# A decode kernel's gate weights of layer 1: three loads of 3, 6 and 3 blocks in place of two of 6 and 6

## The chip, the cores and the metric

One core of one Trainium2 chip. The metric is the device time of one launch in microseconds (us), lower is better.

## The reference

Two layers, each an attention step for one token over the last 4096 positions of a cache (32 heads of 192), and a gated MLP. Both layers use the same weights.

```python
def _B_ref(x, w_gate, w_up, w_down):          # the part that the change touches
    g = jnp.einsum("bsd,df->bsf", x, w_gate)  # D = 640, F = 1536
    u = jnp.einsum("bsd,df->bsf", x, w_up)
    h = _sigmoid(g) * u
    return jnp.einsum("bsf,fd->bsd", h, w_down)

x = x + _A_ref(_layernorm(x), k_cache, v_cache, wq, wo)   # layer 1: attention
x = x + _B_ref(_layernorm(x), w_gate, w_up, w_down)       #          MLP
x = x + _A_ref(...)                                       # layer 2, same weights and cache
x = x + _B_ref(...)
```

## The kernel before

The kernel streams 218 MB from HBM through a large on-chip buffer. All its large loads are issued by SyncE, in one fixed order, on one queue. A load is issued once the instructions that read the old content of its place are done (a semaphore wait on SyncE); later loads wait behind it. So the queue is kept full as long as SyncE is released early enough.

Layer 1's MLP works in a region of cells, each of which holds one block: 128 of the 1536 columns of a weight (128 x 640 values of bfloat16, 160 KB). The gate needs cells 0 to 11, the first seven up blocks cells 12 to 18. The first down blocks and the rest of up are loaded over the gate's cells once the gate's matmuls have read them.

```python
# the gate's matmuls are done in four groups of three blocks: name: (first cell, first block, end block)
MW = {"wg0": (0, 0, 3), "wg1": (3, 3, 6), "wg2": (6, 6, 9), "wg3": (9, 9, 12), "u0": (12, 0, 2), "u1": (14, 2, 7),
      "d0": (0, 0, 3), "d1": (3, 3, 6), "u2": (6, 7, 10), "u3": (9, 10, 12), "d2": (11, 6, 9), ...}
# its loads, in the order in which they are issued: as MW, but the gate in two loads
MD = {"wg0": (0, 0, 6), "wg2": (6, 6, 12), **{k: v for k, v in MW.items() if k[0] != "w"}}
# which group of matmuls must be done before a load into its cells
MAFTER = {"d0": ("wg0",), "d1": ("wg1",), "u2": ("wg2",), "u3": ("wg3",), "d2": ("wg3", "u0"), ...}
# ... the program's order of loads around it:
seq += [("wol", 14), ("wol", 15)] + [(k,) for k in (*MD, "v1", "wq2", "v0", ...)]

# the MLP of layer 1 (cut)
for k in ("wg0", "wg1", "wg2", "wg3"):
    c, f0, f1 = MW[k]
    mark("done_" + k, proj(0, range(f0, f1), g_of, 0, rc[c:c + f1 - f0]))   # waits for the loads of these cells
ln_rstd(K2_MLP, eps_m, rstd_c, res("rstd"))
up("u0", "u1")
# ... sigmoid; then hT = gate * up for the first 7 blocks
down("d0", "d1"); up("u2", "u3")
# ... hT for the last 5 blocks
down("d2", "d3", "d4")
```

`wol14` and `wol15` are the last weights of the attention; `u1` (800 KB) is the last load before `d0`, the first one that has to wait for gate matmuls.

## Time and profile before

| | before |
|---|---|
| time, median of the first three runs | 513.68 us (513.53 to 513.91) |
| span of the profiled run | 512.2 us |
| mean DMA rate | 427 GB/s |
| first up pair landed / first down load issued | 279.80 us / 275.45 us |

The page of the kernel before. The first line is busy time in us, share of the span and instructions of each engine; the line DMA has one digit for each fortieth of the span, the busy share of the sixteen DMA engines in tenths (9 is 90% or more):

```profile
PE 262.5 (51%) x3716; PEld 138.4 (27%) x3716; DVE 101.5 (20%) x385; ACT 85.1 (17%) x171; POOL 4.3 (1%) x31
...
DMA  9999999999999999999999999999999999999996
...
DMA packets 9676, 218.47 MB, mean 427 GB/s; under 512 B 1208, under 2 KB 1592, under 8 KB 4664
```

Every slice but the last reads 9, and 218.47 MB at 427 GB/s make 511.6 us of the span's 512.2. That is the bound: the DMA engines never rest, so the time is the bytes, plus whatever makes an engine rest.

Next, the chain of waits of the kernel before around layer 1's MLP: start, duration, what.

```profile
260.92 18.89 DMA big<-in_wu_dram
...
279.85 0.84 PE scores L684 x25
...
280.71 5.40 DMA big<-in_wd_dram
```

The chain goes through "DMA" from the issue of the second up load at 260.92 to its landing at 279.80. This load did not take 18.9 us; it stood in the queue behind the others for most of them. A chain of waits through a full queue shows what waited, and not what could be made shorter.

The timeline of SyncE, which issues the loads (start, duration from the first to the last of the group, line, output and input, count). "wg" is the gate, "wu" up, "wd" down:

```profile
259.49 0.91 SPq L217 DMA_DIRECT2D big<-in_wg_dram  x2
260.44 0.91 SPq L217 DMA_DIRECT2D big<-in_wu_dram  x2
275.45 0.80 SPq L217 DMA_DIRECT2D big<-in_wd_dram  x2
277.74 0.81 SPq L217 DMA_DIRECT2D big<-in_wu_dram  x2
278.83 2.85 SPq L217 DMA_DIRECT2D big<-in_wd_dram  x3
```

And the timeline of TensorE in the same stretch; L684 is the gate's and up's matmuls, the square bracket gives the idle time before and what ended it:

```profile
274.86 0.96 PE L684 MATMUL scores<-sh,big 128*128 128x1 bf16 x30 [0.61 <-DVE bank L670]
277.15 0.96 PE L684 MATMUL scores<-sh,big 128*128 128x1 bf16 x30 [1.34 <-DMA big<-in_wg_dram]
277.97 0.56 PE L384 MATMUL bank<-sc 128*128 128x1 f32 x2
278.40 0.41 PE L684 MATMUL scores<-sh,big 128*128 128x1 bf16 x10
279.85 0.83 PE L684 MATMUL scores<-sh,big 128*128 128x1 bf16 x25 [1.05 <-DMA big<-in_wu_dram]
```

The gate runs in two bursts of 30 matmuls, one for each load. The first burst releases the first two down loads on SyncE, the second the next loads.

### The profile page before, as it was taken

How to read it: one execution, taken by the hardware profiler on the slowest of the kernel's cores; microseconds unless marked ns; L12 is line 12 of the kernel's file. 1: busy time of each engine (PE TensorE's matmuls, PEld its weight loads, DVE VectorE, ACT ScalarE, POOL GpSimd, SP SyncE). 2: the span in 40 equal slices, each digit the busy share in tenths (PEclk: the TensorE clock that was granted, in tenths of full speed). 3: DMA queues.
4: the chain of work that ended last, by engine and by line, in shares of the span. 5: the costliest groups of instructions: out<-in, count | busy, mean ns of one | idle time of the engine just before them, and what ended most of it. 6: DMA issues, size and time to landing. Idle time of an engine off the chain costs nothing.

```text
span 512.2 us, 8583 instructions
## 1 busy us (share of the span) xinstructions
PE 262.5 (51%) x3716; PEld 138.4 (27%) x3716; DVE 101.5 (20%) x385; ACT 85.1 (17%) x171; POOL 4.3 (1%) x31
## 2 busy tenths in 40 slices
PE   0352455344643254436566767774725344634565
PEld 0221222122311122222234424442312122312234
DVE  0221212112210221112121343231202112210311
ACT  1110111011100111011121024221211011101220
POOL 0010000000000000000000000000000000000000
PEclk9955665565566775566575578675655566555855
DMA  9999999999999999999999999999999999999996
GB/s 426 426 427 426 427 430 428 430 453 444 426 430 430 431 435 426 430 448 444 399 420 412 409 440 434 432 430 427 450 439 435 430 430 439 431 431 413 434 424 280
DMA packets 9676, 218.47 MB, mean 427 GB/s; under 512 B 1208, under 2 KB 1592, under 8 KB 4664
## 3 DMA queue, kind: packets, MB, share of 16 engines
q1 hardware_dynamic: 9512, 218.14, 99.2%
q8 instruction: 13, 0.21, 0.1%
q10 hardware_dynamic: 144, 0.06, 0.0%
q14 instruction: 7, 0.06, 0.0%
HBM read 218.20 MB, written 0.00 MB: 426 GB/s over the span
## 4 chain that ended last, share of the span: by engine, by line
DMA 64%; PE 22%; DVE 8%; ACT 3%; issue 2%; SPq 1%; DVEq 0%; POOL 0%; ACTq 0%; POOLq 0%
DMA big<-in_uc_dram 54%; PE scores L432 8%; DMA big<-in_wd_dram 6%; PE o L494 6%; DMA big<-in_wu_dram 4%; DVE sc L442 3%; PE bank L448 2%; ACT e_sb L458 2%; PE bank L414 2%; PE bank L529 1%; SPq L217 1%; PE bank L464 1%; ACT diag L445 1%; DVE sc L477 1%; DVE qs L420 1%
## 5 line engine op out<-in xcount | busy, mean ns | idle before, releaser
L432 PE MATMUL scores<-big,qs 128*32 128x512 bf16 x744 | 82.0, 608 | 10.3 <-DVE qs L420 9.6
L414 PE MATMUL bank<-sh,big 128*128 128x1 bf16 x465 | 17.0, 166 | 130.9 <-DMA big<-in_uc_dram 128.5
L494 PE MATMUL o<-big,et_sb 128*2 128x384 bf16 x1024 | 77.4, 471 | 8.5 <-DMA big<-in_uc_dram 4.2
L445 ACT ACTIVATE diag<-cst,sc 128x128 f32<-128x128 bf16 x32 | 12.8, 401 | 304.8 <-DVE sc L442 296.8
L442 DVE TENSOR_REDUCE sc<-scores 128x1 f32<-128x1024 f32 x31 | 37.9, 1224 | 77.8 <-PE scores L432 77.8
L414 PEld LDWEIGHTS bank<-sh,big 128*128 128x128 bf16 x465 | 14.6, 103 | 134.0 <-DMA big<-in_uc_dram 112.2
L448 PE MATMUL bank<-diag,sc 128*128 128x128 f32 x64 | 22.5, 447 | 46.7 <-ACT diag L445 46.7
L458 ACT ACTIVATE e_sb<-scores,sc 128x1024 bf16<-128x1024 f32 x31 | 37.4, 1205 | 42.1 <-DVE sc L453 39.9
L494 PEld LDWEIGHTS o<-big,et_sb 128*2 128x2 bf16 x1024 | 28.4, 107 | 44.2 <-issue 29.9
L420 DVE TENSOR_TENSOR qs<-bank,cst 128x96 bf16<-128x96 f32 x30 | 7.7, 258 | 159.6 <-PE bank L414 159.6
L432 PEld LDWEIGHTS scores<-big,qs 128*32 128x32 bf16 x744 | 24.3, 131 | 43.0 <-issue 29.5
L448 PEld LDWEIGHTS bank<-diag,sc 128*128 128x128 f32 x64 | 14.1, 276 | 72.7 <-ACT diag L445 70.4
L501 ACT CAST o_sb<-o 128x384 bf16<-128x384 f32 x64 | 29.7, 474 | 22.7 <-PE o L494 22.4
L529 PE MATMUL bank<-sh,big 128*128 128x1 bf16 x480 | 17.1, 165 | 14.9 <-DVE sh L518 14.9
L468 DVE CAST et_sb<-bank 128x64 bf16<-128x64 f32 x32 | 7.2, 225 | 71.1 <-PE bank L464 71.1
L529 PEld LDWEIGHTS bank<-sh,big 128*128 128x128 bf16 x480 | 14.5, 99 | 17.4 <-DVE sh L518 12.1
L449 DVE TENSOR_REDUCE sc<-bank 128x2 f32<-128x128 f32 x32 | 9.3, 292 | 43.3 <-PE bank L448 43.3
L464 PE MATMUL bank<-cst,e_sb 128*128 128x8 bf16 x256 | 11.7, 169 | 6.8 <-ACT e_sb L458 6.7
L464 PEld LDWEIGHTS bank<-cst,e_sb 128*128 128x128 bf16 x256 | 9.0, 102 | 23.0 <-issue 16.5
L475 PE MATMUL o<-sc 128*128 128x2 f32 x62 | 13.7, 291 | 0.6 <-ACT o_sb L501 0.6
L475 PEld LDWEIGHTS o<-sc 128*128 128x128 f32 x62 | 11.8, 239 | 2.0 <-ACT o_sb L501 1.3
L477 DVE RECIPROCAL sc<-o 64x1 f32<-64x1 f32 x62 | 10.2, 165 | 9.5 <-PE o L475 7.9
(80 smaller groups left out, 109.5 us busy)
## 6 DMA issues: line engine op xcount, KB each, us to landing
big<-in_uc_dram SPq DMA_DIRECT2D x20, 7104.0 KB, 22.6
big<-in_uc_dram SPq DMA_DIRECT2D x11, 3552.0 KB, 20.6
big<-in_uc_dram SPq DMA_DIRECT2D x2, 3072.0 KB, 18.6
big<-in_uc_dram SPq DMA_DIRECT2D x8, 480.0 KB, 7.4
big<-in_uc_dram SPq DMA_DIRECT2D x1, 2784.0 KB, 13.3
big<-in_uc_dram SPq DMA_DIRECT2D x1, 2304.0 KB, 10.7
big<-in_uc_dram SPq DMA_DIRECT2D x1, 2048.0 KB, 12.1
big<-in_wg_dram SPq DMA_DIRECT2D x2, 960.0 KB, 16.2
```

Of the source, the lines that this page charges most:

```text
L414: ins = t.matmul(qe[:, i:i + 1], lhsT=w[:, c * 2 * DH + c0:c * 2 * DH + c0 + P], rhs=xq[:, c:c + 1], start=(c == 0), stop=(c == DC - 1))
L432: ins = t.matmul(sc_x[1 + b][32 * j:32 * j + 32, :], lhsT=qs[:, y, k, :], rhs=slot(sa, WQE + k * W + (4 * b + j) * 512, 512), start=(k == ...
L442: pg.op("dve", lambda v: v.reduce_max(out=mx, in_=sc_x[0][:], axis=AX.X), wr=[res("mx")], ex=sc_x[3:5])
L445: pg.op("act", lambda a: a.mul(out=diag[:], in_=ident, mul=mx), rd=[res("cst"), res("mx")], wr=[res("diag")])
L448: pg.op("pe", lambda t: t.matmul(dmx[:, 0:P], lhsT=ones_f, rhs=diag[:], start=True, stop=True), rd=[res("diag"), res("ones")], ex=[rb[2]])
L458: pg.op("act", lambda a: a.activation(out=e_sb[:], in_=sc_x[0][:], func=ACT.Exp, bias=nbias, scale=srs_c, accum_out=rowsum), rd=[res("nbia ...
L464: ins = t.matmul(qe[:, 0:2 * NB].rearrange("p (r x) -> p r x", r=2)[:, :, 4 * b:4 * b + 4], lhsT=e_sb[:, b * P:(b + 1) * P], rhs=sel, star ...
L475: pg.op("pe", lambda t: t.matmul(sm, lhsT=ones_f, rhs=rs2[z], start=True, stop=True), rd=[res(f"rs2{z}"), res("ones")], wr=[res("rsum")], ...
L477: rb[bk].last["dve"] = pg.op("dve", lambda v, h=h: v.reciprocal(out=Rn[z][64 * h:64 * h + 64], in_=sm[64 * h:64 * h + 64, h:h + 1]), rd=[r ...
L494: ins = t.matmul(o8[h][32 * j:32 * j + 2, 0:2 * DH].rearrange("p (a d) -> p a d", a=2), lhsT=et_sb[:, z, h * NB + 2 * u:h * NB + 2 * u + 2 ...
L501: pg.op("act", lambda a, h=h: a.copy(out=o8_sb[:, :, h * DH:(h + 1) * DH], in_=o8[h][:, 0:2 * DH].rearrange("p (a d) -> p a d", a=2)), wr= ...
L529: ins = t.matmul(yT[:, j:j + 1], lhsT=wo[:, c * D + j * P:c * D + (j + 1) * P], rhs=oTb[z][:, c:c + 1], start=False, stop=(c == 2), skip_g ...
```

## The change

The first gate group (blocks 0 to 2) gets a load of its own, so that its matmuls can start as soon as 480 KB have landed, and the load that they release can be issued earlier. The middle six blocks, read by two groups of matmuls, come in one load, and the last three in another.

```diff
-    MD = {"wg0": (0, 0, 6), "wg2": (6, 6, 12), **{k: v for k, v in MW.items() if k[0] != "w"}}
+    MD = {"wg0": (0, 0, 3), "wg1": (3, 3, 9), "wg3": (9, 9, 12), **{k: v for k, v in MW.items() if k[0] != "w"}}
```

## The prediction

> **What bounds the kernel now.** The DMA engines. The page's DMA table gives 218.47 MB at a mean of 427 GB/s: 511.6 us of a 512.2 us span. Its slices show a DMA share of 9 in all but the last, while PE is busy 51%, DVE 20%, ACT 17%. The DMA packet records say it more sharply: from about 1 to 508 us at least fifteen, nearly always sixteen packets are in flight, also from 255 to 292 us, where the first layer's MLP runs. The largest packets (56,832 B in 2098 ns on one engine, 433 GB/s on sixteen) sit at the "fabric ceiling" of 435 GB/s that the Trainium skill gives ("DMA: Bandwidth & Descriptors", Specifications). The chain of waits shows PE 22% and DVE 8%, but it follows buffers coming free while the queue still holds earlier transfers; those shares can't be won.
>
> **What the change does.** Two gate loads of 960 KB (blocks 0-5, 6-11) of the first layer become 480, 960 and 480 KB (0-2, 3-8, 9-11). Bytes, destinations, arithmetic and matmul order stay. It adds one issue and one semaphore.
>
> 1. Earlier first block. In the list of DMA issues with landings, the first 960 KB land at 274.81 us, the second at 277.11. In the timeline the normalised input is ready near 274.5 and the gate matmuls start at 274.86. With 480 KB landing near 273.7, blocks 0-2 start near 274.5, and the first down load is issued near 275.1 instead of 275.45.
> 2. Blocks 3-5 now wait for the 960 KB piece, near 276.1: the second down load is issued near 276.6 instead of 275.85. The second pair of up loads goes out 0.4 to 0.7 us sooner; the last gate block ends near 277.75 instead of 278.1.
> 3. None of it is on the critical path. The first down load was issued 4.35 us before the transfer ahead of it landed (279.80); that is the smallest such margin among the MLP's released loads (others 4.4 to 6.6 us). Moving issues by -0.7 to +0.8 us never empties the queue. hT waits for the up load that lands at 279.80, behind the same bytes.
> 4. Cost. A packet of 3,840 B takes 149 ns, one of 7,680 B 291 ns: two small ones cost 7 ns more. On each engine eight packets of 7,680 B become sixteen of 3,840 B: 56 ns, plus one semaphore packet of 9 ns: +0.065 us on a saturated resource. The Trainium skill (same page, "Anatomy of one DMA") calls the semaphore write nearly free; 9 ns agrees.
> 5. The extra issue costs SyncE about 0.47 us near 260 us (spacing of neighbouring issues), 15 us before it could matter.
>
> **Predicted time:** 513.68 + 0.07 = 513.75 us, range 513.2 to 514.3 (the three runs spread over 0.4 us). Faster by over 2%: 0.005; within 2%: 0.99; slower: 0.005.
>
> **What would show it.** Right: gate landings near 273.7, 276.1 and 277.3; gate matmuls in three bursts; following up loads landing about 0.07 us later; sixteen packets in flight from 255 to 292 us; 256 more packets of 3,840 B and 128 fewer of 7,680 B. Wrong in step 3: packets in flight well below sixteen there. Wrong in step 4: landings drifting by several tenths.
>
> **What would make it wrong.** A chip with another DMA rate or wider spread; a queue that holds fewer loads than I think, so that one more outstanding load stalls SyncE; the granted clock falling differently in layer 2, so that a buffer comes free later than the queue's slack allows.

## More of the kernel before

Last, stretches of 1 us: for each engine its busy time, then the granted clock of TensorE, the mean busy share of the sixteen DMA engines (it can pass 1, since an engine's packets overlap a little), and GB/s:

```profile
core 0: us, PE busy (x) PEld busy (x) DVE busy (x) ACT busy (x) POOL busy (x), PEclk, DMA share, GB/s
...
277.00:278.00 1.00, 0.85 (x31) 0.85 (x31) 0.00 (x0) 0.00 (x0) 0.00 (x0) 0.50 0.99 401
278.00:279.00 1.00, 0.80 (x17) 0.72 (x13) 0.00 (x0) 0.40 (x2) 0.00 (x0) 0.50 0.99 405
279.00:280.00 1.00, 0.15 (x5) 0.15 (x6) 0.40 (x2) 0.34 (x2) 0.00 (x0) 0.50 1.02 417
280.00:281.00 1.00, 0.68 (x25) 0.59 (x23) 0.23 (x1) 0.00 (x0) 0.00 (x0) 0.50 1.14 362
```

The DMA share stays near 1 through the hand-over from gate to down loads. Single stretches waver in GB/s, but by the packet records at least fifteen packets are in flight at every moment from 255 to 292 us.

## The result, and the profile after

| | before | after |
|---|---|---|
| time, median of six runs | 513.63 us (513.21 to 513.99) | 513.75 us (513.35 to 514.30) |
| ratio | | 1.0003, 95% interval 0.999 to 1.0016 |
| span of the profiled run | 512.2 us | 513.0 us |
| gate landings | 274.81, 277.11 | 273.95, 276.24, 277.40 |
| first up pair landed | 279.80 | 280.13 |
| the four gate releases on SyncE: loads issued | 275.45, 275.85, 277.74, 278.14 | 275.44, 276.87, 277.27, 278.04 |

A ratio here is the mean time of one kernel's fast runs over that of the other's of the same rounds, so it is not quite the ratio of the medians quoted.

The time did not change: the interval goes from 0.1% faster to 0.16% slower. The changed kernel's profiled run happened to be its slowest (514.3 us); a later profile of it has a span of 511.9 us. In the first one the DMA engines were about 0.5 us late (mean of the sixteen) in the load issued at 208 us, well before the MLP, with a stretch near 61 us in which the packets in flight fell to 13. When its numbers are laid beside those of before, some 0.3 us are to be taken off in the MLP: the last attention weights had landed at 272.81 us in place of 272.52.

The page of the changed kernel:

```profile
PE 262.5 (51%) x3716; PEld 137.8 (27%) x3716; DVE 101.6 (20%) x385; ACT 84.8 (17%) x171; POOL 4.2 (1%) x31
...
DMA  9999999999999999999999999999999999999996
...
DMA packets 9820, 218.47 MB, mean 426 GB/s; under 512 B 1224, under 2 KB 1608, under 8 KB 4808
```

The busy times are the same, and the bytes are; there are 144 more packets, which are 128 of data (256 more of 3,840 B, 128 fewer of 7,680 B) and 16 semaphore writes.

Its chain of waits:

```profile
262.05 18.08 DMA big<-in_wu_dram
...
280.18 0.84 PE scores L684 x25
...
281.03 5.94 DMA big<-in_wd_dram
```

The same chain, with the same up load at its middle. The timeline of SyncE:

```profile
260.15 1.38 SPq L217 DMA_DIRECT2D big<-in_wg_dram  x3
261.57 2.69 SPq L217 DMA_DIRECT2D big<-in_wu_dram  x2
275.44 1.76 SPq L217 DMA_DIRECT2D big<-in_wd_dram  x2
277.27 1.09 SPq L217 DMA_DIRECT2D big<-in_wu_dram  x2
278.73 3.10 SPq L217 DMA_DIRECT2D big<-in_wd_dram  x3
```

Three gate loads; the first down load goes out at 275.44 (275.16 without the offset of this run; the second profile has 275.17), and the second not 0.4 but 1.43 us behind it. The timeline of TensorE:

```profile
274.87 0.54 PE L684 MATMUL scores<-sh,big 128*128 128x1 bf16 x15 [0.35 <-DVE sc L374]
276.29 0.96 PE L684 MATMUL scores<-sh,big 128*128 128x1 bf16 x30 [0.87 <-DMA big<-in_wg_dram]
277.45 0.56 PE L684 MATMUL scores<-sh,big 128*128 128x1 bf16 x15 [0.20 <-DMA big<-in_wg_dram]
277.87 0.56 PE L384 MATMUL bank<-sc 128*128 128x1 f32 x2
278.30 0.41 PE L684 MATMUL scores<-sh,big 128*128 128x1 bf16 x10
280.18 0.82 PE L684 MATMUL scores<-sh,big 128*128 128x1 bf16 x25 [1.48 <-DMA big<-in_wu_dram]
```

Three bursts of 15, 30 and 15 matmuls, as the diff says. The first starts when the normalised input is ready. Both timelines name DVE as its releaser, but in the kernel before the load landed at 274.81 us, 0.05 us before the first matmul, and here it landed at 273.95, 0.92 us before: the load is no longer what the burst waits for. The stretches of 1 us:

```profile
277.00:278.00 1.00, 0.80 (x26) 0.71 (x22) 0.00 (x0) 0.00 (x0) 0.00 (x0) 0.50 1.04 431
278.00:279.00 1.00, 0.70 (x13) 0.62 (x12) 0.00 (x0) 0.46 (x2) 0.00 (x0) 0.50 1.00 412
279.00:280.00 1.00, 0.00 (x0) 0.00 (x0) 0.40 (x2) 0.27 (x1) 0.00 (x0) 0.50 1.07 432
280.00:281.00 1.00, 0.82 (x25) 0.74 (x25) 0.00 (x0) 0.00 (x0) 0.00 (x0) 0.50 0.96 388
```

The DMA share stays near 1 (0.96 to 1.07), as before. Whatever the change did to the gate, the DMA engines did not notice.

### The profile page after: what moved, and what is told of

The parts are those of the page before. It is cut to its first block, busy times and chain, and to the rows that moved or that the text cites. A ratio compares the mean times of both kernels' runs of the same rounds, so it can differ in the third digit from the quotient of the medians.

```text
span 513.0 us, 8584 instructions
## 1 busy us (share of the span) xinstructions
PE 262.5 (51%) x3716; PEld 137.8 (27%) x3716; DVE 101.6 (20%) x385; ACT 84.8 (17%) x171; POOL 4.2 (1%) x31
## 4 chain that ended last, share of the span: by engine, by line
DMA 63%; PE 23%; DVE 7%; ACT 2%; issue 2%; SPq 1%; DVEq 0%; POOL 0%; ACTq 0%; POOLq 0%
DMA big<-in_uc_dram 54%; PE scores L432 8%; PE o L494 7%; DMA big<-in_wd_dram 6%; DMA big<-in_wu_dram 4%; DVE sc L442 3%; PE bank L448 2%; PE bank L414 2%; PE bank L529 1%; ACT e_sb L458 1%; PE bank L464 1%; SPq L217 1%; ACT diag L445 1%; DVE sc L477 1%; DVE qs L420 1%
```

## The experiments

Two theories of why the time stayed stood at first.

- **Theory A**: the DMA engines are saturated, and issues come early enough to keep them so. Shifting releases by under 1 us does nothing; only packets cost.
- **Theory B**: the chain of matmuls from the gate to the next layer sets the time, and the change's earlier first group and later second group cancel.
- A third, **theory C**, is that every load carries a fixed cost that the queue does not hide.

Each kernel was timed over five rounds, but for "one load, last" (three), beside the kernel before on the same chip.

| kernel | first down load issued, us | idle DMA time, 270 to 300 us | median | before | ratio (95%) |
|---|---|---|---|---|---|
| before | 275.45 | 0.01 | | | |
| changed, again | 275.17 | 0.01 | 513.78 | 513.88 | 0.9999 (0.9986 to 1.0013) |
| twelve loads | 274.82 | 0.00 | 513.86 | 513.88 | 1.0000 (0.9986 to 1.0014) |
| gate matmuls twice | 275.57 | 0.01 | 514.16 | 513.88 | 1.0004 (0.9991 to 1.0018) |
| three and nine | 275.44 | 0.11 | 513.71 | 514.16 | 0.9988 (0.9976 to 1.0001) |
| nine and three | 276.40 | 0.03 | 513.76 | 514.16 | 0.9990 (0.9977 to 1.0003) |
| gate matmuls four times | 276.96 | 1.74 | 517.69 | 513.90 | 1.0077 (1.0064 to 1.0091) |
| eleven and one | 277.26 | 0.41 | 515.07 | 514.16 | 1.0019 (1.0004 to 1.0034) |
| one load | 277.63 | 0.75 | 515.44 | 513.88 | 1.0032 (1.0018 to 1.0045) |
| one load, last | 280.77 | 3.28 | 518.03 | 514.16 | 1.0076 (1.0059 to 1.0093) |

"Idle DMA time" is worked out from the trace's packet records: the number of packets in flight at every moment, its shortfall below sixteen summed over time and divided by 16. It is a lower bound of what is lost: the mean number in flight of kernels that kept their time is 16.3 to 16.5 in this stretch, not 16, and a packet that takes longer than usual counts as work (the last experiment comes back to this).

### The changed kernel again

The same kernel as the change; no edit.

> The changed kernel itself, once more. Theory A (the DMA engines are saturated at every moment, so only their own packets cost time): 513.75 us within 0.4 us, ratio to the kernel before 1.0001. Theory B (the chain of matmuls from the gate to the next layer sets the time, and an earlier first block and later second block cancel): also about 1.000. This run is the control, and its trace tells whether the 0.65 us by which the first down load landed late in the first trace of the changed kernel is repeatable (it would be 1.8 us after the up load ahead of it again) or jitter between DMA engines (then about 1.2 us).

Measured: 513.78 us against 513.88, ratio 0.9999. Its first down load landed 1.12 us behind the up load ahead of it (280.99 and 279.87), so the 1.84 us of the first trace do not belong to the change. In the first trace the spread between the first and the last engine rose from 1.75 to 2.41 us at this load, and a fetch of instructions (a packet of 16,384 B, 0.93 us) lies there, at 279.82 us. Whether it held up the last engine can't be seen, since the records of packets do not name their engine. The four releases went out at 275.17, 276.59, 276.99 and 277.74 us.

### One gate load

```diff
-    MD = {"wg0": (0, 0, 6), "wg2": (6, 6, 12), **{
+    MD = {"wg0": (0, 0, 12), **{
```

> All twelve gate blocks in one load of 1920 KB, so that no gate matmul can start before about 277.1 us, 2.3 us later than before, and the first down load is issued near 277.7 us in place of 275.45. Theory A: eight packets of 15,360 B (573 ns) per engine in place of sixteen of 7,680 B (291 ns), 72 ns less, and one semaphore packet of 9 ns less: -0.08 us, ratio 0.9998; the smallest margin of a load's issue to the landing ahead of it falls from 4.35 to about 2 us, and at least fifteen packets stay in flight. Theory B: the gate's last block and what follows it end 1 to 2 us later, so +1 to +2 us, ratio 1.002 to 1.004.

Measured: 515.44 us against 513.88, ratio 1.0032: 1.6 us slower, where theory A expected 0.08 us faster and full queues. Theory B had the size right. But the stretches of 1 us say where the time went:

```profile
277.00:278.00 1.00, 0.96 (x36) 0.97 (x37) 0.00 (x0) 0.00 (x0) 0.00 (x0) 0.50 0.89 369
278.00:279.00 1.00, 1.00 (x32) 1.00 (x30) 0.00 (x0) 0.00 (x0) 0.00 (x0) 0.50 0.81 165
279.00:280.00 1.00, 0.77 (x22) 0.69 (x22) 0.00 (x0) 0.67 (x3) 0.00 (x0) 0.50 0.71 210
280.00:281.00 1.00, 0.55 (x21) 0.46 (x18) 0.63 (x3) 0.06 (x1) 0.00 (x0) 0.50 0.96 369
```

From 278 to 280 us the DMA engines moved 165 and 210 GB/s; the packet records fall to four in flight at 278.25. So it is idle DMA time after all, though SyncE issued the first down load at 277.63 us, 2.04 us before the load ahead of it landed (279.67).

The records of the semaphores explain it. A load adds 16 to its semaphore, one from each DMA engine when that engine's share is in; the Trainium skill says so ("DMA: Bandwidth & Descriptors", Why a DMA increments its semaphore by 16 and not by 1: the engines "finish independently"), and the trace has 16 separate times. For the up load ahead:

```
second up load, times of its 16 increments (us)   first    4th     8th    12th    13th    last
before                                           277.89  278.06  278.18  278.59  279.25  279.80
changed, again                                   277.95  278.16  278.28  278.53  279.46  279.87
one load                                         277.95  278.08  278.25  278.54  279.41  279.67
```

"Landed" is the last engine. Twelve of the sixteen had finished more than 1 us before it. The spread stays nearly the same from load to load (1.90 to 2.05 us for the loads that land from 262.95 to 282.16 us in the kernel before). The records do not name the engines, so it is inferred, and not seen, that an engine that is ahead stays ahead; that one runs dry first. In the kernel before, the first down load's packets begin at 277.58 us, which is when the first engine was through with the up load. And in "one load" the first down packets begin at 278.59, 0.96 us after their issue at 277.63. So the condition is: issue about 1 us before the first engine runs dry, that is by about 276.6 us.

- **Theory A2** therefore: as A, but a release has to come by 276.6 us; the margin of the kernel before is 277.58 - 275.45 - 0.96 = 1.17 us, not the 4.35 us that the prediction counted to the landing.

### Twelve gate loads

```diff
-    MD = {"wg0": (0, 0, 6), "wg2": (6, 6, 12), **{
+    MD = {**{f"wg{i}": (i, i, i + 1) for i in range(12)}, **{
```

> Twelve gate loads of 160 KB, one block each. Gate matmuls start as early as they can, and each block waits for 160 KB only. Theory A: 96 packets of 1,280 B (55 ns) per engine, 5280 ns, in place of 4656 ns, and ten semaphore packets of 9 ns more: +0.71 us, ratio 1.0014; the loads behind land about 0.7 us later. Theory B: no slower than before, perhaps 0.3 us faster, ratio 0.9994 to 1.0000. Theory C (every load carries a fixed cost of its own that the queue does not hide, of the order of 0.5 us as the issues on SyncE are spaced): +4 to +5 us, ratio 1.009.

Measured: 513.86 us against 513.88. Theory C is out: ten more loads cost nothing near 4 us. The 0.71 us of theory A lie at the edge of the interval (0.14% is 0.72 us), so the runs alone can't decide and the trace has to. Over the mean of the sixteen increments, the second up load comes 0.45 us later behind twelve loads than behind two, with the times just ahead of the gate loads as the zero; for the change itself it is 0.05 to 0.06 us in both of its traces. So packet durations, taken one by one, over-count: 0.45 of 0.71 us. The traces have 16.3 to 16.5 packets in flight on sixteen engines, so packets overlap a little; that this is what hides a part of each was not tested. SyncE was held up for 3.1 us at the fifth of these issues and for 2.5 at the sixth, with no cost, since the queue in front of the engines was long.

### Every gate matmul twice

```diff
-  mark("done_" + k, proj(0, range(f0, f1), g_of, 0, rc[c:c + f1 - f0]))
+  mark("done_" + k, proj(0, [*range(f0, f1)] * 2, g_of, 0, rc[c:c + f1 - f0]))
```

This is made from the changed kernel; the second pass overwrites the first with the same values.

> The changed kernel with every gate matmul done twice: 60 more matmuls of 128x1, about 0.54 us more for every three blocks, right result. The first down load is issued near 275.7, the last of the four gate releases near 279 to 280 us. Theory A: the added 2.2 us lie inside the margins of 4.35 us and more: ratio 1.000 (within 0.0007) to the kernel before. Theory B: +1 to +2 us, ratio 1.002 to 1.004.

Measured: 514.16 us against 513.88, ratio 1.0004: no effect that the runs can show, and the DMA idle time stayed at 0.01 us. Here is TensorE's timeline with each gate matmul done twice:

```profile
274.60 0.94 PE L684 MATMUL scores<-sh,big 128*128 128x1 bf16 x30 [0.35 <-DVE sc L374]
276.01 2.56 PE L684 MATMUL scores<-sh,big 128*128 128x1 bf16 x90 [0.48 <-DMA big<-in_wg_dram]
278.44 0.57 PE L384 MATMUL bank<-sc 128*128 128x1 f32 x2
```

and with one gate load, with SyncE's issue of its first two down loads:

```profile
277.04 1.76 PE L684 MATMUL scores<-sh,big 128*128 128x1 bf16 x60 [3.03 <-DMA big<-in_wg_dram]
278.66 0.56 PE L384 MATMUL bank<-sc 128*128 128x1 f32 x2
277.63 0.80 SPq L217 DMA_DIRECT2D big<-in_wd_dram  x2
```

The gate ends at 276.01 + 2.56 = 278.57 us in the first and at 277.04 + 1.76 = 278.80 us in the second. These are 0.23 us apart, and the second kernel lost 1.6 us and the first at most 0.9. What tells them apart is the first release: 275.57 against 277.63 us. That speaks against theory B; the next experiment tests it more sharply.

### Three and nine

```diff
-    MD = {"wg0": (0, 0, 6), "wg2": (6, 6, 12), **{
+    MD = {"wg0": (0, 0, 3), "wg1": (3, 3, 12), **{
```

> Two gate loads, blocks 0-2 and blocks 3-11. The last gate blocks become ready at about 277.1 us, as with one load, but the first down load is issued near 275.2, as in the changed kernel. Theory A2 (formed after the one-load kernel lost 1.6 us: the sixteen DMA engines reach the end of a load up to 2 us apart, the first of them near 277.6 us, and about 1 us passes from an issue to its first packets, so the first down load must be issued by about 276.5): sixteen packets stay in flight, ratio 1.000 within 0.001. Theory B (the end of the gate matmuls sets the time): the gate ends within 0.4 us of the one-load kernel's, so +1.2 to +1.6 us, ratio 1.0025 to 1.003.

Measured: 513.71 us against 514.16, ratio 0.9988 (0.9976 to 1.0001); B's 1.0025 to 1.003 is excluded. The first down load went out at 275.44 us, the second only at 278.01; the packets in flight fell to 13 near 279.75 us, 0.11 us in all. TensorE's last gate matmuls, and SyncE's issue of the first two down loads:

```profile
277.42 1.36 PE L684 MATMUL scores<-sh,big 128*128 128x1 bf16 x45 [2.01 <-DMA big<-in_wg_dram]
275.44 2.89 SPq L217 DMA_DIRECT2D big<-in_wd_dram  x2
```

The gate ends at 277.42 + 1.36 = 278.78 us, with one load at 278.80: the same end, and only the kernel with the late first release lost time. A late gate alone costs nothing.

### Nine and three

```diff
-    MD = {"wg0": (0, 0, 6), "wg2": (6, 6, 12), **{
+    MD = {"wg0": (0, 0, 9), "wg3": (9, 9, 12), **{
```

> Two gate loads, blocks 0-8 and 9-11. The first down load is issued near 276.6 us, 1.1 us later than before, and the gate matmuls end as early as in the changed kernel. Theory A2: 276.6 + 1.0 = 277.6 is just the time at which the first engines run out: no loss or up to 0.3 us, ratio 1.000 to 1.0006. Theory B: no loss.

Measured: 513.76 us against 514.16, ratio 0.9990. The release at 276.40 us was just in time: packets in flight dipped to 14 near 277.75 us, 0.03 us in all.

### Eleven and one

```diff
-    MD = {"wg0": (0, 0, 6), "wg2": (6, 6, 12), **{
+    MD = {"wg0": (0, 0, 11), "wg4": (11, 11, 12), **{
```

> Two gate loads, blocks 0-10 and block 11. The first down load is issued near 277.35 us. Theory A2: the first engines stand idle for 0.6 to 0.8 us, and the loss lies between those of nine and three and of one load: +0.5 to +1.4 us, ratio 1.001 to 1.0027, with in-flight packets falling below eight near 278 us. Theory B: the gate ends about 0.3 us earlier than with one load: +1.2 us. This run alone does not tell A2 from B; it gives the third point of the curve.

Measured: 515.07 us against 514.16, ratio 1.0019, about 0.9 us slower. The release at 277.26 was followed by the first packets at 278.22, again 0.96 us later, and the packets in flight fell to six. The third point lies on the curve: 276.40 no loss, 277.26 about 1 us, 277.63 about 1.6 us.

### One gate load, behind the up loads

```diff
-    MD = {"wg0": (0, 0, 6), "wg2": (6, 6, 12), **{
+    MD = {"wg0": (0, 0, 12), **{
-seq += [("wol", 14), ("wol", 15)] + [(k,) for k in (*MD, "v1", ...
+seq += [("wol", 14), ("wol", 15)] + [(k,) for k in ("u0", "u1", *(k for k in MD if k not in ("u0", "u1")), "v1", ...
```

> One gate load, put behind the two up loads, so that it is the last transfer before the down loads. Gate matmuls start when it lands, near 279.8 us; the first down load is issued near 280.4. Theory A (margins counted to the landing of the load ahead, and 1 us to the first packet): the queue is empty for about 1.6 us: +1.6 us. Theory A2 (engines run out from 277.6 on): most engines idle from about 277.7 to 281.3, the last four from 279.4: +2.5 to +3.6 us, ratio 1.005 to 1.007.

Measured: 518.03 us against 514.16, ratio 1.0076, 3.9 us slower: more than theory A's 1.6 us, and 0.3 us over A2's range (the interval of the ratio, 1.0059 to 1.0093, reaches into it). The stretches of 1 us show the engines running dry one after another and then all being empty:

```profile
278.00:279.00 1.00, 0.00 (x0) 0.00 (x0) 0.00 (x0) 0.00 (x0) 0.00 (x0) 0.50 0.47 200
279.00:280.00 1.00, 0.00 (x0) 0.00 (x0) 0.00 (x0) 0.00 (x0) 0.00 (x0) 0.50 0.07 31
280.00:281.00 1.00, 0.82 (x31) 0.82 (x31) 0.00 (x0) 0.00 (x0) 0.00 (x0) 0.50 0.00 0
281.00:282.00 1.00, 1.00 (x37) 1.00 (x34) 0.00 (x0) 0.00 (x0) 0.00 (x0) 0.50 0.47 70
282.00:283.00 1.00, 1.00 (x32) 1.00 (x32) 0.00 (x0) 0.53 (x3) 0.00 (x0) 0.50 0.70 219
```

Engines begin to stop at 277.75 us and the last one does so near 279.75, a spread of 2 us on the way out; the first down load, issued at 280.77, has its first packets at 281.72, 0.95 us later.

### Every gate matmul four times

The edit is that of "twice" with 4 in place of 2.

> The changed kernel with every gate matmul done four times, right result. The gate loads land as in the changed kernel; only the releases move: the first down load is issued near 276.8 us, the second near 279.0, the up loads near 281.1 and 283.3. Theory A2 (first engines run out near 277.6, 278.9, 281.1 and 283.2 us, 1 us from issue to first packets): small gap at the first down load, then about 0.9 us on most engines at each of the next three releases, idle of some 2.4 us of all sixteen engines, +2.3 to +3.5 us, ratio 1.0045 to 1.007. Theory B (the end of the gate matmuls sets the time): the gate ends 5.4 us later than in the changed kernel, so about +5.4 us, ratio 1.0105. No effect would say that issue times do not matter and that the one-load kernel lost its time to something else.

Measured: 517.69 us against 513.90, ratio 1.0077 (1.0064 to 1.0091): 3.8 us slower, 0.3 us above A2's range, into which the interval reaches, and 1.6 us below B's figure, which it excludes. The gate loads land as in the changed kernel, so lateness of the matmuls alone makes the DMA engines idle: there are gaps near 280.2, 282.2 and 284.4 us, behind the issues at 278.56, 281.34 and 282.94, with eight, five and eight packets in flight at their lowest. Two things were not in the estimate. TensorE stood for 1.04 us ahead of its last gate matmuls without a wait that the profile shows. And about 1 us from issue to packets is no constant: the load issued at 282.94 had its first packets at 284.33, 1.39 us later and not 0.96, and the one issued at 278.56 came 1.23 us before the first engine was through with the load ahead of it (its first increment, 280.10, less 0.31 us), and yet engines ran dry. Twice was free and four times was not: it is a threshold, as A2 says and B does not.

In both "four times" and "one load" the lost time exceeds the idle time as counted (3.8 against 1.74 us, 1.6 against 0.75). In the traces the loss is complete by the layer-2 loads that land from 296 us on: there the mean of the sixteen increments is 2.0 us ("one load") and 4.6 us ("four times") behind the changed kernel's second trace, of which 0.3 us stood before the gate in the latter, and it neither grows nor shrinks by more than 0.3 us in the 200 us that follow. The packet records of the same traces show most of what is missing. A packet of 3,840 B mostly takes 0.149 us (the median in the kernel before); where the first down load of "one load" begins, from 278.59 us on, such packets take up to 1.10 us, and the count takes their engines for busy. What the packets of 277 to 300 us took beyond the usual for their size, summed and divided by 16, is set beside the idle time of the same stretch:

| kernel | idle, us | excess of packets, us | both, less the 0.61 of the kernel before | lost, us |
|---|---|---|---|---|
| eleven and one | 0.41 | 0.98 | 0.8 | 0.9 |
| one load | 0.75 | 1.44 | 1.6 | 1.6 |
| gate matmuls four times | 1.74 | 2.49 | 3.6 | 3.8 |
| one load, last | 3.28 | 1.16 | 3.8 | 3.9 |

For the kernels that kept their time both make 0.1 to 0.6 us, so a figure of this sum is good to some 0.3 us. So a late release costs the time that engines stand idle and slow packets besides; why these packets are slow no run here shows.

## Why the prediction was right

The prediction was 513.75 us, and 513.75 us were measured; the run-to-run spread of 1 us says that this much agreement is luck, and that "no change" is the finding.

1. *What bounds it*: right. The packets in flight stay at fifteen or more from 255 to 292 us before and after, and the kernels in which they did so, or in which they fell no lower than 13 for a moment, kept their time. In the four in which they fell to six or lower, the time rose.
2. *First block earlier, second later* (steps 1 and 2): right to 0.2 us, in the second trace or once the offset of the first is taken off. Predicted landings 273.7, 276.1, 277.3; in the second trace 273.66, 275.95, 277.10. Predicted releases 275.1 and 276.6; measured 275.17 and 276.59. The gate's end was predicted near 277.75; it came at 277.45 + 0.56 = 278.01 us in the first trace, 277.73 without the offset.
3. *None of it on the critical path* (step 3): right in its conclusion, and wrong in its size. "Issued 4.35 us before the transfer ahead of it landed" is no margin, because a landing is the last of sixteen engines, and because about 1 us passes from issue to packets. The margin at the first down load is 1.17 us before. The change moves the first release 0.3 us forward and the second 0.7 us back. For the second, the same sum can be estimated: an engine's increment comes 0.31 us after it has gone on to the next load (277.89 against 277.58), so in the changed kernel's second trace, where the first down load's first increment is at 279.13, the margin is 279.13 - 0.31 - 276.59 - 0.96 = 1.27 us. So it holds, with about 1 us to spare and not with four. (With the 1.39 us that "four times" once showed in place of 0.96, 0.7 and 0.8 us would be left.) "One load", 2.2 us later than before at the first release, is inside the margin that the prediction counted, and lost 1.6 us.
4. *Cost in packets* (step 4): +0.065 us predicted, 0.05 to 0.06 us in the mean of the sixteen increments in both traces; runs alone, with 1 us of spread, can't show it. The sum behind it over-counts when it is large (0.45 of 0.71 us with twelve loads). The Trainium skill calls the semaphore write nearly free ("DMA: Bandwidth & Descriptors", Anatomy of one DMA, which tells of loads issued by GpSimd); sixteen more writes of 9 ns on sixteen engines agree, for loads issued by SyncE.
5. *The extra issue* (step 5): the last issue of the group kept SyncE 2.2 us in both traces and not 0.47. So the extra load did stall SyncE, which the prediction had named among what would make it wrong. It had no cost, because the next load was to be issued 11 us later. What held it was not tried.

## What to carry to other kernels

Where the DMA engines are saturated, as here, splitting a load to let compute start earlier gained nothing; what the compute owed them was only the next issue, early enough. Count that margin from the issue to the time when the *first* DMA engine runs dry, less the time from an issue to its packets, and not to the landing of the load ahead; and leave some of it, since the time from issue to packets was 0.96 us in some places here and 1.39 in another. The way to see it is to delay the release in steps: nothing happens up to a point (276.40 us here), and further delays cost (0.9 us at 277.26, 1.6 at 277.63).

## What the Trainium skill lacked or had wrong

- "DMA: Bandwidth & Descriptors" says that the engines of one DMA finish independently, but no page says how far they drift apart in a long run on one queue: 1.6 to 3.3 us between the first and the last increment of one load in the kernel before (0.8 us for the first loads), nearly the same from each load to the next but for a few jumps. The margin of an issue depends on it.
- The same page (Specifications) gives about 0.6 us to the first byte for loads issued by SyncE. From the start of the issue to the first packet on dry engines it was 0.95 to 0.96 us in three kernels here and 1.39 us in a fourth. The two may not count from the same moments.
- The same page (Bandwidth, measured on loads issued by GpSimd) advises 1 MiB or more per load and calls transfers under 64 KB descriptor-dominated; it has no figure for a row of loads on a full queue. Here twelve loads of 160 KB in a row took 4.90 us (272.43 to 277.33), 401 GB/s: the fixed time of a load is hidden, and only some 5 to 6 ns per added packet remain (0.45 us for 80 more packets of data, 90 with the semaphore writes, on each engine).
- "Runtime: NRT & Kernel Launch" (Instruction fetch mechanics) has fetches of 16 KiB on a queue of the sequencer's own and calls their cost mostly hidden. It lacks what they do to a kernel bound by DMA: the kernel before has 13 such packets of 16,384 B, about 0.9 us each, three of them between 280 and 303 us. Around two of them (33.46 and 289.23 us) the spread between the first and the last engine rose from 0.84 to 1.81 us and from 1.74 to 3.26 us from one load to the next; that the fetch took this time from one engine's data is likely, but was not tested.
- No page has it that packets are slow where a queue has run dry and stays short of loads: up to 1.10 us for 3,840 B in "one load", in place of 0.149.
